# A fused attention and gated-MLP kernel: weights' high words through a leaky ReLU without a sign step, two constants in one array, products split, and a new order of issue

## The chip, the cores and the metric

The kernel runs on one core of a Trainium2 chip. The core has engines that run side by side, each with a queue of its own that is worked off in order: TensorE (PE in the profile, with PEld for its weight loads), VectorE (DVE), ScalarE (ACT), GpSimd (POOL) and SyncE (SP), which here issues nearly all DMA transfers. The metric is the time of one execution on the device in microseconds (us); lower is better.

## The reference

What is computed, for 8 batches, 8 heads, 576 positions and a head width of 64:

```python
k_p = k.reshape(B, H, 72, 8, D).mean(axis=3)          # keys and values pooled by 8
v_p = v.reshape(B, H, 72, 8, D).mean(axis=3)
attn = softmax(q @ k_p.transpose(...) / sqrt(D))
x = attn @ v_p                                         # -> (8, 576, 512)
h = gelu_tanh(x @ w_in)                                # w_in: 512 x 1024
u, v = h[..., :512], h[..., 512:]
v_n = (v - mean(v)) / sqrt(var(v) + 1e-6) * g_ln
v_s = einsum('ts,bsd->btd', w_sg, v_n) + b_sg[None, :, None]
out = x + (u * v_s) @ w_out
```

`w_in` and `w_out` come as 64-bit floats, everything else as 32-bit floats.

## The kernel before

Each product of two 32-bit operands is made of three products of their parts: an operand is rounded to a high part (`wih`, `xhl[:, 0]`, `ghi`, `vhh`) and the remainder is its low part (`wil`, `xhl[:, 1]`, `glo`, `vhl`), and high by high, high by low and low by high are added up in PSUM. The steps have letters. For batch b: A, B, C, E load keys, values, queries and leftovers; K and P pool keys and values; S makes the scores of one pair of heads (tile `e`: maximum `nmax`, exponential, sum `ssum`, division); L and T turn the scores round; V makes the attention output (tiles `x32` and `xhl`); H makes the v half of the first product (five row tiles), its gelu and its normalisation; J does the first four row tiles of H for batch 0, column group by column group; U makes the u half; W the product with `w_sg` (`wsh`, `wsl`) and the gate; O the last product; Z the store. "S1+3" in the text is step S of head pair 1, batch 3.

For batch 0 TensorE turns the scores (L176). For later batches VectorE transposes them in blocks (L509), the blocks go to HBM (`tfar`) and come back in rows (tile `al`), ScalarE rounds them to `ah` (L558), VectorE makes the remainder in `al` (L561), and V multiplies. There is one `al` buffer, so the load for the next head pair starts when V of this one is done.

Before batch 0 can be multiplied, the weights have to be split. Those of 64 bits are taken apart with integer operations (`step_w`): ScalarE scales the high word, read as a float, into `top` (L275), VectorE shifts it left by three bits (L277), puts the sign bit back (L278) and masks (L279); ScalarE casts it to the high part (L283), and L222, L224, L228 and L231 make the low part. There are twelve such steps (v0 to v3, u0 to u3, o0 to o3), each of a tile of 128x512. `load_wsg` loads `w_sg`, `b_sg` (copied to all partitions, `bbc`) and `g_ln` (`gcol`).

The list ORDER sets the order in which the steps are recorded, and with it each engine's queue: a name there advances that step to its next yield. The set OTHER names single operations that go to another engine than the usual one (a sum to VectorE instead of GpSimd, a copy to VectorE instead of ScalarE, the scores' exponential as one instruction after a subtraction on VectorE instead of ten with a bias each). Matmul outputs turn over two PSUM tiles `mps` and two `aps`.

Of the kernel before, what the change touches and what calls it, by code (L numbers as in the profile page):

```python
# [32 lines left out]
V1+0 S0+1 o0 P1+1 H1+0 V3+0 S1+1 V2+0 E0+1 H2+0 o1 A1+2 V0+0 S0+1 S0+1 H0+0 H0+0 S1+1 H3+0 H1+0 H4+0 S2+1 S1+1 S0+1
H0+0 H2+0 H3+0 S2+1 H1+0 o1 S3+1 lo1 H1+0 H1+0 o1 o1 o2 H4+0 H4+0 s3 C0+2 P2+1 P2+1 U0+0 U0+0 H4+0 K0+2 S2+1 H4+0
H3+0 o3 U1+0 U2+0 U1+0 U2+0 P2+1 o2 H3+0 S0+1 o2 H3+0 H2+0 H4+0 H2+0 o3 o2 U3+0 U3+0 S2+1 T0+1 H2+0 S3+1 S2+1 C1+2
T0+1 H4+0 o3 H3+0 S3+1 o3 H4+0 S1+1 S1+1 W0+0 W0+0 K1+2 K1+2 S3+1 W0+0 S3+1 B0+2 C3+2 T1+1 P0+2 L0+1 W1+0 P2+1 C2+2
K0+2 L0+1 W2+0 S0+2 T0+1 W1+0 W1+0 W1+0 W2+0 W2+0 S0+2 W0+0 S1+2 S0+2 L0+1 P2+1 B1+2 T0+1 W2+0 W3+0 A0+3 W3+0 W3+0
# [798 lines left out]
```

## Time and profile before

| What | us |
|---|---|
| median of three runs | 558.33 |
| lowest and highest | 555.67, 558.74 |
| the profiled execution | 558.14 |
| its span, first to last instruction | 556.4 |

So 1.74 us of the profiled execution lie outside its span. TensorE is busy for 531.2 us of the span (95%), VectorE for 420.4, ScalarE for 278.8, GpSimd for 239.6. The page's slices of the span show TensorE at 90% or more in nearly all of them from 140 us to the end, and below that in the first quarter.

### The profile page before, as it was taken

How to read it: one execution, taken by the hardware profiler on the slowest of the kernel's cores; microseconds unless marked ns; L12 is line 12 of the kernel's file. 1: busy time of each engine (PE TensorE's matmuls, PEld its weight loads, DVE VectorE, ACT ScalarE, POOL GpSimd, SP SyncE). 2: the span in 40 equal slices, each digit the busy share in tenths (PEclk: the TensorE clock that was granted, in tenths of full speed). 3: DMA queues.
4: the chain of work that ended last, by engine and by line, in shares of the span. 5: the costliest groups of instructions: out<-in, count | busy, mean ns of one | idle time of the engine just before them, and what ended most of it. 6: DMA issues, size and time to landing. Idle time of an engine off the chain costs nothing.

```text
span 556.4 us, 9530 instructions
## 1 busy us (share of the span) xinstructions
PE 531.2 (95%) x3552; PEld 500.6 (90%) x3552; DVE 420.4 (76%) x674; ACT 278.8 (50%) x569; POOL 239.6 (43%) x323
## 2 busy tenths in 40 slices
PE   3998889999999999999999999999999999999996
PEld 3976689987999999989999999989999899989996
DVE  5688999778879779787777987885878956574262
ACT  3696999455764649343554537354354354313100
POOL 4331658477366753564333642562524532232000
PEclk9998999989999999999999999999999999999998
DMA  8993304655734345325534065441341242101002
GB/s 298 339 325 96 141 2 137 192 150 138 250 100 103 88 145 205 95 64 161 152 87 135 0 184 155 132 144 46 104 130 47 44 126 89 42 1 65 1 0 107
DMA packets 43134, 67.08 MB, mean 121 GB/s; under 512 B 5776, under 2 KB 22160, under 8 KB 43088
## 3 DMA queue, kind: packets, MB, share of 16 engines
q1 hardware_dynamic: 42800, 66.03, 39.0%
q8 instruction: 28, 0.46, 0.3%
q10 hardware_dynamic: 288, 0.44, 0.2%
q14 instruction: 18, 0.15, 0.1%
HBM read 47.73 MB, written 18.73 MB: 119 GB/s over the span
## 4 chain that ended last, share of the span: by engine, by line
PE 82%; ACT 6%; DVE 5%; DMA 4%; issue 1%; SPq 1%; POOL 1%; DVEq 0%; ACTq 0%
PE mps L133 68%; PE aps L133 13%; DMA qT<-in_q 1%; DMA al<-tfar 1%; DMA kraw<-in_k 1%; ACT e L457 1%; ACT L204 1%; SPq L234 1%; DVE al L561 1%; PE aps L176 1%; DVE wsl L231 0%; ACT vg L640 0%; DVE y L509 0%; ACT top L275 0%; ACT kbd L377 0%
## 5 line engine op out<-in xcount | busy, mean ns | idle before, releaser
L133 PE MATMUL mps<-xhl,wih 128*128 128x288 f32 x512 | 89.1, 295 | 2.7 <-ACT u L681 1.7
L133 PE MATMUL mps<-wih,xhl 128*128 128x512 f32 x256 | 84.2, 399 | 0.1
L133 PEld LDWEIGHTS mps<-xhl,wih 128*128 128x128 f32 x512 | 75.0, 188 | 4.1 <-ACT u L681 2.0
L443 POOL TENSOR_TENSOR e<-e,ssum 128x720 f32<-128x720 f32 x23 | 36.1, 1570 | 52.4 <-DVE ssum L442 52.3
L133 PEld LDWEIGHTS mps<-wih,xhl 128*128 128x128 f32 x256 | 48.0, 188 | 11.6 <-DVE xhl L231 0.6
L133 PE MATMUL mps<-wsh,vhh 128*128 128x288 f32 x256 | 54.8, 295 | 0.0
L133 PE MATMUL mps<-wsl,vhh 128*128 128x288 f32 x256 | 54.7, 294 | 0.0
L133 PE MATMUL mps<-wsh,vhl 128*128 128x288 f32 x256 | 54.5, 294 | 0.0
L133 PE MATMUL mps<-xhl,wil 128*128 128x288 f32 x256 | 54.5, 294 | 0.0
L133 PE MATMUL mps<-ghi,woh 128*128 128x288 f32 x240 | 52.0, 298 | 0.0
L133 PE MATMUL mps<-glo,woh 128*128 128x288 f32 x240 | 51.2, 294 | 0.0
L133 PE MATMUL mps<-ghi,wol 128*128 128x288 f32 x240 | 51.1, 294 | 0.0
L133 PE MATMUL mps<-wil,xhl 128*128 128x512 f32 x128 | 50.6, 395 | 0.0
L647 POOL TENSOR_TENSOR rstd<-mv,eps 128x1 f32<-128x1 f32 (+1 forms) x40 | 13.1, 328 | 76.5 <-DVE mv L645 67.3
L133 PE MATMUL aps<-kbd,qT 128*128 128x144 f32 x300 | 42.7, 292 | 2.7 <-ACT e L457 1.9
L204 ACT ACT_TABLE_LOAD x35 | 44.9, 1283 | 0.6
L133 PEld LDWEIGHTS aps<-kbd,qT 128*128 128x128 f32 x300 | 40.5, 196 | 4.2 <-ACT e L457 2.3
L695 DVE SCALAR_TENSOR_TENSOR mps<-mps,gcol,bbc 128x576 f32<-128x576 f32 x32 | 26.1, 816 | 23.1 <-PE mps L133 23.1
L640 ACT ACTIVATE vg<-mps 128x512 f32<-128x512 f32 x32 | 19.1, 596 | 48.1 <-PE mps L133 43.5
L133 PEld LDWEIGHTS mps<-xhl,wil 128*128 128x128 f32 x256 | 41.0, 188 | 0.0
L133 PEld LDWEIGHTS mps<-wsh,vhl 128*128 128x128 f32 x256 | 40.9, 188 | 0.0
L133 PEld LDWEIGHTS mps<-wsh,vhh 128*128 128x128 f32 x256 | 40.9, 188 | 0.0
(170 smaller groups left out, 1319.1 us busy)
## 6 DMA issues: line engine op xcount, KB each, us to landing
qT<-in_q SPq DMA_DIRECT2D x31, 288.0 KB, 4.4
out<-x SPq DMA_DIRECT2D x31, 288.0 KB, 2.7
kraw<-in_k SPq DMA_DIRECT2D x14, 576.0 KB, 4.5
al<-tfar SPq DMA_DIRECT2D x28, 288.0 KB, 2.9
vraw<-in_v SPq DMA_DIRECT2D x14, 512.0 KB, 5.0
tfar<-y SPq DMA_DIRECT2D x56, 80.0 KB, 1.9
raw<-in_moe_w_in SPq DMA_DIRECT2D x4, 1024.0 KB, 9.5
tfar<-y SPq DMA_DIRECT2D x56, 64.0 KB, 1.8
```

The costliest lines, as they stand in the source:

```text
L133: nc.tensor.matmul(o, lhsT, rhs, start=start, stop=stop)
L176: nc.tensor.transpose(ps[:rows, i * P:(i + 1) * P], src(i), ident if i < NT - 1 else swap)
L204: nc.scalar.activation(early, eps[:, 0:1], func)
L234: queue.dma_start(o, i)
L443: (nc.gpsimd if key in OTHER else nc.vector).tensor_tensor(e, e, rec.unsqueeze(3).broadcast_to([P, NT, 2, SP]), op=ALU.mult)
L457: nc.scalar.activation(e[:, i, h], slots[i][:, h], AF.Exp, bias=nmax[:, i, h:h + 1], accum_out=ssum[:, i, h:h + 1])
L561: nc.vector.tensor_tensor(lo, al, ah.bitcast(F32), op=ALU.subtract)
L640: nc.scalar.activation(vg, o, AF.Gelu_apprx_tanh)
L647: nc.gpsimd.tensor_tensor(rstd, mv[:, 1:2], eps[:n, 1:2], op=ALU.add)
L695: nc.vector.scalar_tensor_tensor(vs, vs, gcol[:, d:d + 1], bbc.rearrange("p (a n) -> p a n", a=2), op0=ALU.mult, op1=ALU.add)
```

## The change

1. In `step_w` the scaling on ScalarE becomes a leaky ReLU (`Prelu`) whose slope for negative inputs is 2^32 times the other. The exponent then carries a bit that the shift by three puts where the sign belongs, so the sign step on VectorE is left out. The cast to the high part may go to GpSimd (`move`).
2. `b_sg` and `g_ln` come in one array (`bg`), already copied to 128 partitions, by one DMA instead of two.
3. The remainder of V (`rest`) may be made on VectorE straight from PSUM; before it was always made from the copy `x32`.
4. J makes high by high and low by high first, for all four row tiles, and high by low (`wil`) after a yield.
5. The last product of the last batch goes to two PSUM tiles instead of one, and each half is added to x right behind its matmuls.
6. ORDER and OTHER are new.

```diff
 ORDER = """
-lv0 A0+0 v0 v0 E0+0 A1+0 C0+0 v1 v1 v1 v1 v0 K0+0 lv1 B0+0 K0+0 A0+1 v3 v0 v2 S0+0 S0+0 K1+0 v3 v2 C1+0 S0+0 K1+0 v3
+C0+0 E0+0 A0+0 K0+0 K0+0 lv0 v0 C1+0 S0+0 S1+0 v0 S0+0 v1 S1+0 v0 v1 v0 A1+0 S0+0 C2+0 B0+0 S1+0 S0+0 K1+0 K1+0 B1+0
...
-    bbc = const.tile([P, S], F32, name="bbc")
-    gcol = const.tile([P, DF2 // P], F32, name="gcol")
+    both = const.tile([P, S + DF2 // P], F32, name="both")
+    bbc, gcol = both[:, 0:S], both[:, S:]
...
+    def rest(lo, x, ps, hi, key):
+        if key in OTHER:
+            nc.vector.tensor_tensor(lo.rearrange("p (a n) -> p a n", a=2), ps,
+                                    hi.rearrange("p (a n) -> p a n", a=2), op=ALU.subtract)
+        else:
+            nc.gpsimd.tensor_tensor(lo, x, hi, op=ALU.subtract)
...
-            nc.scalar.activation(top.bitcast(F32), high.bitcast(F32), AF.Copy, scale=2.0 ** -112)
+            nc.scalar.activation(top.bitcast(F32), high.bitcast(F32), AF.Prelu, scale=2.0 ** -112, alpha=2.0 ** 32)
             yield
             nc.vector.tensor_scalar(top, top, 3, None, op0=ALU.logical_shift_left)
-            nc.vector.scalar_tensor_tensor(top, high, -0x80000000, top, op0=ALU.bitwise_and, op1=ALU.bitwise_or)
             nc.vector.tensor_scalar(high, top, -0x800000, None, op0=ALU.bitwise_and)
...
-            nc.scalar.copy(hi, top)
+            move(hi, top, f"{name}{c}h")
...
-        load(bbc, b_sg.rearrange("(o t) -> o t", o=1).broadcast_to([P, S]))
-        load(gcol, g_ln.rearrange("(c p) -> p c", p=P))
+        load(both, bg)
...
-        combine(xhl[:, 1, g], x32, xhl[:, 0, g].bitcast(F32), ALU.subtract, f"V{min(b, 3)}{g}")
+        rest(xhl[:, 1, g], x32, xs, xhl[:, 0, g].bitcast(F32), f"V{min(b, 3)}{g}")
...
-        for i, o in enumerate(st["hp"]):
-            t = slice(i * P, i * P + P)
-            for j, (w, x) in enumerate(((wih, 0), (wil, 0), (wih, 1))):
-                mm(o, xhl[:, x, c, t], w[:, c, DF2:2 * DF2], c == 0 and j == 0, c == KC - 1 and j == 2)
-        yield
+        for pairs in (((wih, 0), (wih, 1)), ((wil, 0),)):
+            for i, o in enumerate(st["hp"]):
+                t = slice(i * P, i * P + P)
+                for w, x in pairs:
+                    mm(o, xhl[:, x, c, t], w[:, c, DF2:2 * DF2], c == 0 and w is wih and x == 0, c == KC - 1 and w is wil)
+            yield
...
-        ps = atile() if b == B - 1 and m % 2 else mtile()
...
             for n in range(2):
                 t = slice(HALF * n, HALF * (n + 1))
+                ps = (atile, mtile)[n]()[:, 0, 0:HALF]
...
-            for n in range(2):
-                nc.vector.tensor_tensor(x[:, n], ps[:, n, 0:HALF], x[:, n], op=ALU.add)
+                nc.vector.tensor_tensor(x[:, n], ps, x[:, n], op=ALU.add)
                 yield
             return
+        ps = atile() if b == B - 1 and m % 2 else mtile()
```

Three places show what the new order does. The first is SyncE's queue at the start; `raw` from `in_moe_w_in` is a piece of `w_in`, `kraw` are keys, `raw0` takes the leftover keys (`in_kv0`) and the values (`in_v0`) of batch 0. Before:

```order
L234 DMA raw_123<-in_moe_w_in 128x2x1024
L234 DMA kraw_125<-in_k0 128x1024
L234 DMA raw0_132<-in_kv0 64x1024
L234 DMA kraw_135<-in_k0 128x1024
L234 DMA raw_160<-in_moe_w_in 128x2x1024
L234 DMA raw0_132<-in_v0 128x1024
L234 DMA kraw_165<-in_k 128x1152
L234 DMA qT_201<-in_q 128x576
```

Now:

```order
L242 DMA raw0_124<-in_kv0 64x1024
L242 DMA kraw_127<-in_k0 128x1024
L242 DMA raw_142<-in_moe_w_in 128x2x1024
L242 DMA qT_146<-in_q 128x576
L242 DMA kraw_180<-in_k0 128x1024
L242 DMA qT_183<-in_q 128x576
L242 DMA raw0_124<-in_v0 128x1024 x2
L242 DMA raw_227<-in_moe_w_in 128x2x1024
```

The leftover keys and the first half of the keys have moved ahead of the first piece of `w_in`, and both halves of the values ahead of its second piece.

The second place is TensorE's queue at J0+0, the first products with `w_in`. Before, from S3+0 on:

```order
L133 MATMUL aps<-kbd_96,qT 128x144 x5
L133 MATMUL aps<-ah,vb 128x288
L133 MATMUL aps<-lt,vl 128x288
L133 MATMUL aps<-ah,vb 128x288
L133 MATMUL aps<-lt,vl 128x288
L133 MATMUL mps<-wih,xhl 128x512
L133 MATMUL mps<-wil,xhl 128x512
L133 MATMUL mps<-wih,xhl 128x512 x2
```

Now, from the second turn (T1+0) on:

```order
L177 MATMUL aps<-ident,e 128x128 x4
L177 MATMUL aps<-swap,e 128x128
L134 MATMUL mps<-wih,xhl 128x512 x8
L134 MATMUL aps<-ah,vb 128x288
L134 MATMUL aps<-lt,vl 128x288
L134 MATMUL aps<-ah,vb 128x288
L134 MATMUL aps<-lt,vl 128x288
```

The eight matmuls with `wih` come first, V1+0 (the four rows with `ah` and `lt`) has moved behind them, and the four matmuls with `wil` come later still.

The third place is TensorE's queue at the end of W3+0, where V of batch 1 begins (`vbh`, `vbl` are its values). Before:

```order
L133 MATMUL mps<-wth,vht 128x288 x2
L133 MATMUL mps<-wtl,vht 128x288 x2
L133 MATMUL mps<-ghi,woh 128x288 x2
L133 MATMUL mps<-ghi,wol 128x288 x2
L133 MATMUL mps<-glo,woh 128x288 x2
```

Now:

```order
L134 MATMUL mps<-wth,vht 128x288 x2
L134 MATMUL mps<-wtl,vht 128x288 x2
L134 MATMUL aps<-ah,vbh 128x288
L134 MATMUL aps<-ah,vbl 128x288
L134 MATMUL aps<-lt,vl 128x288
L134 MATMUL aps<-al,vbh 128x288
```

V0+1 has moved ahead of the first chunks of O0+0 (18 matmuls with `ghi` and `glo`), which now stand between it and V1+1: 42 matmuls there, against 30 before.

## Rows read from the trace of the kernel before

**Rows 1.** Stages: us; busy (instructions) of PE, PEld, DVE, ACT, POOL; clock, DMA share, GB/s.
```profile
8.56:38.72 30.16, 28.42 (x137) 25.08 (x138) 24.00 (x43) 20.56 (x72) 8.48 (x8) 1.00 0.98 351
38.72:69.60 30.88, 26.37 (x129) 20.71 (x127) 28.14 (x46) 25.57 (x75) 12.64 (x14) 0.94 0.42 132
69.60:85.10 15.50, 13.33 (x96) 12.87 (x97) 14.28 (x30) 15.36 (x41) 9.07 (x12) 1.00 0.01 2
85.10:128.90 43.80, 40.91 (x293) 39.74 (x292) 36.80 (x51) 25.43 (x74) 28.90 (x30) 0.96 0.58 170
128.90:551.20 422.30, 422.21 (x2902) 402.20 (x2901) 314.54 (x504) 189.28 (x307) 174.32 (x234) 1.00 0.34 100
551.20:556.40 5.20, 0.00 (x0) 0.00 (x0) 0.82 (x2) 0.00 (x0) 0.00 (x0) 0.71 0.46 170
```

**Rows 2.** Timeline of TensorE: start, duration, instructions; in brackets the idle time before.
```profile
38.72 0.61 PE L133 MATMUL mps<-wih,xhl 128*128 128x512 f32 x1
...
69.60 0.80 PE L133 MATMUL mps<-xhl,wih 128*128 128x288 f32 x4 [0.49 <-ACT vg L640]
...
85.11 0.42 PE L133 MATMUL mps<-wsh,vhh 128*128 128x288 f32 x2
```

**Rows 3.** Waits of TensorE from 38.7 to 129 us: total, times, longest.
```profile
PE aps L176 <- DVE e L443: 2.0, 1, 2.0
PE aps L133 <- ACT e L457: 1.9, 1, 1.9
PE aps L133 <- ACT ah L558: 1.8, 1, 1.8
PE mps L133 <- ACT u L681: 1.7, 1, 1.7
```

**Rows 4.** Stages again, as in 1: the two stretches with a low clock.
```profile
43.90:48.40 4.50, 4.47 (x20) 3.50 (x21) 4.40 (x7) 1.31 (x3) 1.62 (x2) 0.62 0.54 175
...
112.40:116.00 3.60, 3.40 (x14) 3.18 (x15) 3.08 (x6) 2.93 (x6) 1.40 (x1) 0.59 0.05 6
```

**Rows 5.** Chain that ended last, at the start: start, duration, what.
```profile
8.56 4.74 PE mps L133 x20
```

**Rows 6.** Timeline of ScalarE at the start, columns as in 2.
```profile
6.15 0.68 ACT L275 ACTIVATE top<-raw 128x512 f32<-128x512 f32 x1 [4.07 <-DMA raw<-in_moe_w_in]
```

**Rows 7.** Groups of VectorE: instructions xcount | busy us, mean ns | idle before.
```profile
L733 DVE TENSOR_TENSOR x<-mps,x 128x576 f32<-128x576 f32 x30 | 22.4, 749 | 15.6 <-PE mps L133 15.4
...
L231 DVE TENSOR_TENSOR xhl<-x,xhl 128x576 fp32r<-128x576 f32 x17 | 15.1, 888 | 2.6 <-ACT x L211 2.4
...
L278 DVE SCALAR_TENSOR_TENSOR top<-raw,top 128x512 int32<-128x512 int32 x12 | 8.3, 693 | 0.4
```

**Rows 8.** Groups of ScalarE, columns as in 7.
```profile
L204 ACT ACT_TABLE_LOAD x35 | 44.9, 1283 | 0.6
...
L453 ACT ACTIVATE e<-e 128x720 f32<-128x720 f32 x25 | 19.8, 801 | 7.5 <-DVE e L448 7.2 <-POOL kraw L358 0.2
...
L457 ACT ACTIVATE e<-aps,nmax 128x72 f32<-128x72 f32 x60 | 18.2, 335 | 0.6 <-DVE nmax L486 0.6
...
L275 ACT ACTIVATE top<-raw 128x512 f32<-128x512 f32 x12 | 7.8, 672 | 4.5 <-DMA raw<-in_moe_w_in 4.5
```

**Rows 9.** Chain that ended last, from 104 to 130 us, columns as in 5.
```profile
106.73 4.90 DMA al<-tfar
...
112.44 0.77 DVE al L561
...
116.93 2.38 PE mps L133 x18
...
122.42 2.98 DMA al<-tfar
...
126.18 1.73 DVE al L561
```

**Rows 10.** Timeline of VectorE at the end, columns as in 2.
```profile
551.23 0.82 DVE L721 TENSOR_TENSOR x<-aps,x 128x288 f32<-128x288 f32 x2 [2.40 <-PE aps L133]
```

More of the change, by code (lines that the diff above doesn't have):

```diff
@@ L33 @@
[L33 to L37, printed above, removed]
@@ new lines @@
+S2+2 T2+1 T3+1 S1+2 V1+1 O1+0 O1+0 S1+2 V0+1 S2+2 O2+0 O2+0 C1+3 T2+1 S0+2 V2+1 A1+3 K1+3 S2+2 O3+0 O3+0 V2+1 V2+1
+V2+1 O2+0 T3+1 T3+1 T3+1 B0+2 S3+2 S0+2 V3+1 P0+2 V3+1 O3+0 T0+2 C0+3 V3+1 H0+1 S2+2 T1+2 S3+2 H0+1 H0+1 S3+2 S3+2
+H1+1 H1+1 H1+1 B1+3 Z0+0 H0+1 V1+1 H2+1 H3+1 H0+1 T0+2 A0+3 H2+1 H1+1 H0+1 H3+1 H1+1 V3+1 H4+1 H1+1 T0+2 H2+1 S2+2
+Z2+0 U0+1 H4+1 H4+1 U0+1 H4+1 H3+1 T0+2 T3+2 S3+2 P2+2 U1+1 K0+3 K0+3 L0+2 P2+2 H2+1 H3+1 H4+1 H2+1 Z3+0 S0+3 S0+3
+U1+1 U2+1 H3+1 H3+1 P2+2 L0+2 P2+2 U3+1 U2+1 P1+3 Z1+0 H2+1 L0+2 L0+2 V0+2 T1+2 S1+3 C3+3 T2+2 H4+1 U3+1 H4+1 H4+1
@@ new lines @@
+S1+3 T1+2 T1+2 V0+2 W0+1 W0+1 V1+2 V1+2 T2+2 S0+3 C2+3 L0+2 T2+2 W1+1 V0+2 W1+1 K1+3 W2+1 E0+3 T2+2 V2+2 S0+3 C0+4
+S2+3 S1+3 W3+1 W1+1 T3+2 V2+2 V1+2 V1+2 W2+1 W1+1 V2+2 T3+2 T3+2 V3+2 B0+3 S1+3 W3+1 W0+1 W0+1 V3+2 V3+2 H0+2 H1+2
+H0+2 V0+2 T0+3 S2+3 P0+3 T0+3 H1+2 W2+1 W2+1 W3+1 O0+1 A1+4 W3+1 O0+1 C1+4 H1+2 S3+3 O1+1 O0+1 O1+1 H0+2 P2+3 S0+3
+O2+1 A0+4 S3+3 H0+2 V2+2 S2+3 P2+3 V3+2 K1+4 H1+2 H1+2 O2+1 H1+2 O1+1 S3+3 B1+4 H2+2 K1+4 K0+4 O2+1 S2+3 S3+3 Z2+1
+H2+2 P2+3 B0+4 H0+2 H0+2 H3+2 S1+3 K0+4 H4+2 H2+2 S0+4 H3+2 T1+3 U0+2 S2+3 H4+2 H4+2 S3+3 C3+4 U1+2 H3+2 L0+3 H4+2
@@ new lines @@
+T0+3 P2+3 H4+2 S1+4 S0+4 U0+2 U1+2 Z0+1 P2+3 H2+2 H2+2 H4+2 O3+1 H2+2 L0+3 L0+3 O3+1 P0+4 L0+3 A0+5 T0+3 H3+2 V0+3
+T1+3 T1+3 U2+2 U2+2 O3+1 H3+2 Z3+1 T2+3 H3+2 S0+4 S1+4 T1+3 U3+2 U3+2 V1+3 T2+3 L0+3 Z1+1 H4+2 T2+3 H4+2 W0+2 T3+3
+P1+4 V0+3 V0+3 T2+3 E0+4 W0+2 W1+2 V2+3 V1+3 S0+4 T3+3 C1+5 W1+2 W0+2 K0+5 K0+5 W0+2 S1+4 W1+2 T3+3 T3+3 W2+2 W2+2
+W3+2 W3+2 W1+2 C2+4 V3+3 V2+3 S2+4 V3+3 V3+3 W2+2 V1+3 V2+3 H0+3 W2+2 C0+5 H0+3 S2+4 S2+4 V1+3 S3+4 H0+3 S1+4 H1+3
+H1+3 H2+3 T0+4 H0+3 O0+2 H2+3 S1+4 T0+4 S0+4 H0+3 H0+3 S3+4 T1+4 W3+2 H3+3 H1+3 S3+4 W3+2 O0+2 H3+3 O0+2 H2+3 S0+5
@@ L90, with tile_pooled_attn_gmlp @@
+p20 p21 p31 s0d s3d s4d u0a u0d u0m u1a u1d u1m u2a u2m u3d u3h u3m v0a v1m v2h v2m x22 z13 z20 z21 z22 z23 z24 z31
+z32 z34
 """.split())
 @with_exitstack
-def tile_pooled_attn_gmlp(ctx: ExitStack, tc: tile.TileContext, q, k0, kv0, v0, k, v, vleft, w_in, g_ln, w_sg, b_sg, w_out, out):
+def tile_pooled_attn_gmlp(ctx: ExitStack, tc: tile.TileContext, q, k0, kv0, v0, k, v, vleft, w_in, w_sg, bg, w_out, out):
     nc = tc.nc
@@ L462, in total, with root @@
             nc.vector.tensor_reduce(out=ssum, in_=e, axis=AX.X, op=ALU.add)
+    def root(rstd, var, key):
+        n = rstd.shape[0]
+        nc.gpsimd.tensor_tensor(rstd, var, eps[:n, 1:2], op=ALU.add)
+        nc.gpsimd.tensor_tensor(rstd, rstd, mhalf[:n], op=ALU.pow)
     def scaled(vg, mv, rstd, key):
@@ L646, in step_H @@
         rstd = per.tile([P, 1], F32, name="rstd", tag=f"rstd{i}")[:n]
-        nc.gpsimd.tensor_tensor(rstd, mv[:, 1:2], eps[:n, 1:2], op=ALU.add)
-        nc.gpsimd.tensor_tensor(rstd, rstd, mhalf[:n], op=ALU.pow)
+        root(rstd, mv[:, 1:2], f"r{min(b, 3)}{i}")
         yield
```

98 lines of the change are left out of this document (44 added, 54 removed).

## The prediction

> **What bounds the kernel now.** I read the stages first. From 128.9 us to the last matmul at 551.2 us TensorE is busy for 422.21 of 422.30 us at a granted clock of 1.00 (2.4 GHz) [rows 1]: there its own work is the time, and the change leaves every matmul in place (3345 before and now by the order). So the change can only win ahead of 128.9 us and behind 551.2 us. Ahead of it, the first matmul starts at 8.56 us [rows 5], J0+0 at 38.72, U0+0 at 69.60 and W0+0 at 85.11 [rows 2]. TensorE is idle for 30.16 - 28.42 = 1.74 us between the first matmul and J0+0, for 4.51 us from there to U0+0, for 2.17 to W0+0 and for 2.89 to 128.9 [rows 1]. I read next what ended those waits: 2.0 us for VectorE's division of e ahead of T, 1.9 for ScalarE's exponentials ahead of S, 1.7 for ScalarE's gelu of u, 1.8 for `ah` of V1+1 [rows 3]. Two of these, of 2.0 and 1.8 us, are followed by a stretch with the clock at its lower level (1.2 GHz) for a part: 0.62 over 4.50 us and 0.59 over 3.60 us [rows 4], which costs another 0.38 x 4.50 = 1.7 and 0.41 x 3.60 = 1.5 us. Last I looked at who is full: between J0+0 and W0+0, 46.4 us, VectorE is busy for 28.14 + 14.28 = 42.4 us (91%) and ScalarE for 25.57 + 15.36 = 40.9 (88%) [rows 1]. TensorE waits there for two engines that are nearly full themselves.
>
> **The change, part by part.** The sum is made against the profiled execution, 558.14 us, of which 1.74 lie outside the span; the median of the runs is 558.33, so the two can be taken as the same.
>
> Start. The first matmuls need the leftover keys (256 KB), the first half of the keys (512 KB), and S0+0 needs the query (288 KB). Before, 1024 KB of `w_in` stood ahead on SyncE's queue and landed by 6.15 us [rows 6]; the keys came behind them, at 8.56 [rows 5]. Now these 1056 KB come first. They are as much as that first transfer, so I take 6.3 us: a gain of 2.3 us (1.5 to 2.5). `w_in` comes later, but its high part is wanted by J0+0 only, some 28 us on, and its first piece now has one piece of 1056 KB in front instead of none, at 351 GB/s [rows 1] a delay of 3 us: hidden by those 28. The values now land ahead of the second piece of `w_in`, which c = 2 wants, behind J1.
>
> Up to J0+0 VectorE loses six sign steps, 6 x 0.693 = 4.2 us [rows 7] of its 24.00 [rows 1], and J0 begins with eight matmuls that don't want `wil`. Of the 1.74 us idle I take back 1.2 (0 to 1.7). Together **-3.5 us** at J0+0, with equal work in front. V1+0 has moved behind it, so the record will show J0+0 about a microsecond earlier still.
>
> From J0+0 to W0+0. By TensorE's waits alone, 2.0 + 1.9 + 1.7 us and the clock's 1.7 could go, 7.3 in all; against it J0's second matmul now wants the low part of x, which stands on VectorE behind a sum of keys (`kp`), so I put 1.6 us back: 46.4 - 5.7 = 40.7 us. But VectorE alone has more to do than that. It loses the other six sign steps there, 4.2 us [rows 7]; by the order it gets two sums of keys, two row sums and some steps of the splits that stood ahead of J0+0 before, and gives up two scalings and two remainders of vg and the remainders of P2+1, each of 0.4 to 1.3 us, which I estimate at 3.5 us more, net. That leaves 42.4 - 4.2 + 3.5 = 41.7 us. At its share of now, 91%, the stage takes 45.8 us (-0.6); at 97%, 43.0 (-3.4). ScalarE has slack: 20 of the exponentials with a bias go, 20 x 18.2/60 = 6.1 us, for two whole ones of 0.80, and two of the table loads of 1.283 move behind W0+0 [rows 8]. I take the middle of VectorE's two, **-2.0 us**.
>
> The price of the new ScalarE form: its row is the scaling with Copy, 0.672 us x12 [rows 8], same shape and operands, and I take it unchanged. The program has 38 table loads instead of 36 and none beside the new form. The Trainium skill (ScalarE: Activation LUTs, section Table sets: the hidden batching unit) says that cheap functions such as relu, copy, identity and abs are in every table set; it does not name the leaky ReLU, so by its list a load could be wanted each time. The Trainium skill (ScalarE activation tables: per-element evaluation and per-set limits, section What a function is on this engine) give 1283 ns a load, and the row agrees with 1283. That case is a rival below.
>
> Remainder of V from PSUM: 13 of 32 go that way. No row shows it; its nearest is the sum x<-mps,x of the same size with one operand in PSUM, 0.749 us, against 0.888 for xhl<-x,xhl [rows 7]; so 0.70 to 0.89, and I take 0.75. It need not wait for the copy to x. The cast of a high part on GpSimd (two of twelve) has no row: between 0.3 and 1.4 us, hidden, since the first product with that part comes several microseconds later. The Trainium skill (GPSIMD Engine Reference, section 1. Specifications) says that GpSimd shares its SBUF interfaces with VectorE, with contention for VectorE instructions with two SBUF inputs. By this the form from PSUM would win 13 x 0.139 = 1.8 us of VectorE, and the twelve operations that GpSimd gains ahead of W0+0 would lengthen VectorE's others; the mean of 0.888 beside 0.749 agrees with the first, no row here shows the second.
>
> One DMA instead of two for the constants costs nothing: they are first wanted by the gate of W0+0.
>
> From W0+0 to 128.9. V0+1's end lets the load of `al` go at 106.73; the remainder is ready at 112.44 + 0.77 = 113.2: 6.5 us. For the third it is 122.42 to 127.9, 5.5 us [rows 9]. Eighteen matmuls take 2.38 us [rows 9], 0.132 each: the 30 matmuls behind V0+1 hide 4.0 us, the 42 of now 5.5. So the first wait falls from about 2.5 to 1.0 us, and I take the clock's fall behind it as gone for the most part, 1.3 of 1.5 (a wait of 1.7 us for u has a clock of 1.00 all through its stage [rows 1, 3]). The waits at the other two I leave. **-2.8 us** (-4.2 to +1).
>
> From there to the last matmul there is nothing to win; for the two table loads and the moved work I add **+0.5 us** (0 to +4).
>
> The end. Both additions of the last product now wait for TensorE's end (idle 2.40 us) and take 0.82 us together [rows 10]; stores queue behind the first half's. Now the first half is added 18 matmuls sooner, its store and the others go out while TensorE works, and one half and one small store remain of the 5.20 us [rows 1]. One addition less is 0.4 us, the queue less I estimate at 0.9: **-1.3 us** (-0.4 to -1.8).
>
> Sum: -3.5 - 2.0 - 2.8 + 0.5 - 1.3 = -9.1 us, 558.14 - 9.1 = **549.0 us**.
>
> **Rivals.** *More comes through* (16%): VectorE reaches 97%, the idle time before J0+0 goes, all of V's waits go, no loss later: -4.2 - 3.4 - 4.2 - 1.8 = -13.6, 544.5 us; for it, TensorE's clock would not fall at all. *VectorE stays the bound* (15%): GpSimd has twelve more operations ahead of W0+0 and VectorE waits for its results or is slowed by it, so W0+0 comes where it came, at 85 us; then -2.8 + 0.5 - 1.3 = -3.6, 554.5 us. For it: 91% now; against it, twelve sign steps less. *Slower: a wait at each change of batch* (6%). TensorE has no slack from 128.9 on. If the new order put a result too late there, each idle stretch of 2.0 us with the clock's 1.7 behind it costs 3.7 us; from the third of seven batches on, the gain of 9.1 is gone, and with all seven it is 549.0 + 26 = 575 us. Against it: the PSUM tiles turn over there in the same pattern as before, and VectorE was busy for 314.5 of 422 us. *The leaky ReLU wants its own table* (2%): two loads for each of twelve steps, 24 x 1.283 = 30.8 us on ScalarE, which has 76.5 - 61.5 = 15.0 us idle from the first matmul to W0+0 [rows 1]: 549.0 + 15.8 = 565 us. Against it: the program has no such loads.
>
> **How the numbers follow.** The forecast, 546 to 553 us, has 61%, and the four rivals 16, 15, 6 and 2. The range of 8 in 10 reaches into the first two rivals: 541.5 to 555.0 us. A measurement of this kernel tells 0.5% (2.8 us) from no change, so faster means below 555.5: forecast and first rival and about half of the second, 0.84; same 0.08; slower 0.08.
>
> **What would show it.** The first matmul at 6.0 to 6.6 us; J0+0 near 34; W0+0 near 79.5; the new activation at 0.67 us with no load beside it; the remainder from PSUM at 0.70 to 0.76; VectorE at 93 to 95% between J0+0 and W0+0; under 1.5 us of wait at V1+1 and no low clock there; the stretch from V3+1 to the last matmul within 2 us of 422; 4 us from the last matmul to the end. W0+0 at 83 us or later, or idle time of TensorE behind 130 us, would make it wrong.

## The result and the profile after

The changed kernel takes 551.9 us (median; 551.1 to 552.1) against 558.33 (555.67 to 560.25) of the kernel before: a ratio of 0.989 with a 95% interval of 0.9855 to 0.9925, so 1.1% faster, and inside the 546 to 553 us that I forecast. Its profiled execution took 552.02 us with a span of 550.3; that is 6.1 us less than the profiled execution before, where I had forecast 9.1.

The stages first, cut at the same places as [rows 1]: first matmul, J0+0, U0+0, W0+0, first product of batch 1, last matmul. Columns: us; busy (instructions) of PE, PEld, DVE, ACT, POOL; granted clock, DMA share, GB/s.

```profile
0.00:7.85 7.85, 0.00 (x0) 0.03 (x1) 0.21 (x1) 1.49 (x2) 6.15 (x26) 1.00 0.71 222
7.85:38.09 30.24, 27.30 (x129) 24.10 (x130) 20.25 (x30) 15.41 (x44) 11.73 (x12) 0.89 0.72 277
38.09:67.34 29.25, 26.54 (x139) 21.04 (x137) 27.25 (x48) 25.24 (x60) 18.03 (x22) 1.00 0.71 232
67.34:81.60 14.26, 13.30 (x100) 12.84 (x98) 12.78 (x27) 14.17 (x40) 10.14 (x13) 1.00 0.07 26
81.60:120.25 38.65, 37.53 (x282) 36.79 (x281) 33.23 (x51) 23.87 (x88) 18.37 (x21) 1.00 0.48 139
120.25:546.15 425.90, 424.91 (x2914) 403.77 (x2912) 311.52 (x496) 215.67 (x437) 143.41 (x205) 1.00 0.34 102
546.15:550.30 4.15, 0.00 (x0) 0.00 (x0) 0.46 (x1) 0.00 (x0) 0.00 (x0) 1.00 0.60 225
```

Two pieces of work stand in another stage than before, and have to be taken out before stages are compared. V1+0 is now behind J0+0; it takes 43.10 - 41.16 = 1.9 us. One S step, ten matmuls (1.1 us), is now behind the first product of batch 1. TensorE's timeline (start, duration, instructions, idle time before):

```profile
7.85 1.86 PE L134 MATMUL mps<-pool,kraw 128*128 128x16 f32 x8 [7.85 <-DMA kraw<-in_k]
...
38.09 0.49 PE L134 MATMUL mps<-wih,xhl 128*128 128x512 f32 x1
39.43 1.89 PE L134 MATMUL mps<-wih,xhl 128*128 128x512 f32 x7 [0.85 <-DVE xhl L236]
41.16 0.65 PE L134 MATMUL aps<-ah,vb 128*128 128x288 f32 x2
...
43.10 0.60 PE L177 MATMUL aps<-ident,e 128*128 128x128 f32 x4
...
81.60 0.43 PE L134 MATMUL mps<-wsh,vhh 128*128 128x288 f32 x2
```

With that, the steps of the forecast against the profile (before: [rows 1, 2]; its first product of batch 1 is at 128.73 us, and the steps are rounded to 0.1):

| Step | worked out | forecast | measured |
|---|---|---|---|
| up to J0+0 | 38.09 + 1.9 - 38.72 | -3.5 | +1.3 |
| J0+0 to W0+0 | (43.51 - 1.9) - 46.39 | -2.0 | -4.8 |
| W0+0 to the first product of batch 1 | (38.65 + 1.1) - 43.62 | -2.8 | -3.9 |
| from there to the last matmul | (425.90 - 1.1) - 422.47 | +0.5 | +2.3 |
| last matmul to end | 4.15 - 5.20 | -1.3 | -1.05 |
| sum | | -9.1 | -6.1 |

So the sum was 3 us off, and it hides two larger misses at either end (the start and the steady part, 6.6 us together) that two middle steps made good in part (3.9 us). TensorE's waits ahead of 120 us (total, times, longest) show both sides:

```profile
PE aps L134 <- ACT kbd L383: 1.9, 1, 1.9
PE mps L134 <- ACT vg L652: 0.9, 1, 0.9
PE mps L134 <- ACT u L692: 0.9, 1, 0.9
PE mps L134 <- DVE xhl L236: 0.8, 1, 0.8
...
PE aps L134 <- DMA qT<-in_q: 0.7, 1, 0.7
PE aps L134 <- DVE lt L551: 0.4, 1, 0.4
```

The four waits of 1.7 to 2.0 us of [rows 3] are gone: the gelu of u costs 0.9 instead of 1.7, the division ahead of T and the exponentials ahead of S after J0+0 nothing, and `ah` of V1+1 nothing, with a clock of 1.00 from 38 us to the end. What is new is a wait of 1.9 us for `kbd`, ahead of J0+0.

The three single operations I had priced came out as priced. Groups of ScalarE and VectorE (count | busy us, mean ns | idle before):

```profile
L205 ACT ACT_TABLE_LOAD x37 | 47.5, 1283 | 0.6
...
L283 ACT ACTIVATE top<-raw 128x512 f32<-128x512 f32 x12 | 7.9, 670 | 0.6 <-POOL wil L232 0.5
...
L236 DVE TENSOR_TENSOR xhl<-aps,xhl 128x576 fp32r<-128x576 f32 x13 | 9.7, 745 | 2.0 <-ACT x L212 2.0
```

The leaky ReLU takes 0.670 us (Copy 0.672, [rows 8]) and no table load stands beside any of the twelve; the record has 37 loads against 35, and it has 37 too with the Copy put back (next section), so the two more come with the order. The remainder from PSUM takes 0.745 us (0.75 assumed).

### The profile page after: what moved, and what is told of

The parts are those of the page before. It is cut to its first block, busy times and chain, and to the rows that moved or that the text cites. A ratio compares the mean times of both kernels' runs of the same rounds, so it can differ in the third digit from the quotient of the medians.

```text
span 550.3 us, 9577 instructions
## 1 busy us (share of the span) xinstructions
PE 529.6 (96%) x3552; PEld 498.6 (91%) x3552; DVE 405.7 (74%) x651; ACT 295.9 (54%) x668; POOL 207.8 (38%) x295
## 4 chain that ended last, share of the span: by engine, by line
PE 77%; ACT 8%; DVE 6%; DMA 5%; issue 2%; SPq 1%; POOL 0%; DVEq 0%; ACTq 0%
PE mps L134 66%; PE aps L134 11%; ACT e L463 2%; DMA al<-tfar 1%; SPq L242 1%; ACT L205 1%; DMA kraw<-in_k 1%; DMA vraw<-in_v 1%; DMA qT<-in_q 1%; DVE al L572 1%; ACT vg L482 1%; DVE kp L361 1%; DVE vp L361 1%; DVE nmax L497 1%; ACT vhh L212 1%
## 5 line engine op out<-in xcount | busy, mean ns | idle before, releaser
L134 PE MATMUL mps<-wih,xhl 128*128 128x512 f32 x256 | 81.6, 398 | 0.8 <-DVE xhl L236 0.8
L239 POOL TENSOR_TENSOR xhl<-x,xhl 128x576 fp32r<-128x576 f32 x19 | 27.8, 1469 | 79.3 <-ACT x L212 79.3
L134 PE MATMUL mps<-ghi,woh 128*128 128x288 f32 x244 | 53.5, 299 | 0.0
L449 POOL TENSOR_TENSOR e<-e,ssum 128x720 f32<-128x720 f32 x23 | 33.1, 1437 | 52.1 <-DVE ssum L448 46.9
L134 PE MATMUL mps<-ghi,wol 128*128 128x288 f32 x244 | 52.5, 295 | 0.0
L134 PE MATMUL mps<-wil,xhl 128*128 128x512 f32 x128 | 48.8, 397 | 0.0
L472 POOL TENSOR_TENSOR rstd<-mv,eps 128x1 f32<-128x1 f32 (+1 forms) x40 | 11.0, 274 | 98.5 <-DVE mv L657 93.4
L134 PEld LDWEIGHTS aps<-kbd,qT 128*128 128x128 f32 x300 | 40.3, 194 | 4.4 <-ACT kbd L383 2.0
L706 DVE SCALAR_TENSOR_TENSOR mps<-mps,both 128x576 f32<-128x576 f32 x32 | 26.1, 816 | 20.0 <-PE mps L134 19.9
```

The costliest lines, as they stand in the source:

```text
L134: nc.tensor.matmul(o, lhsT, rhs, start=start, stop=stop)
L239: nc.gpsimd.tensor_tensor(lo, x, hi, op=ALU.subtract)
L449: (nc.gpsimd if key in OTHER else nc.vector).tensor_tensor(e, e, rec.unsqueeze(3).broadcast_to([P, NT, 2, SP]), op=ALU.mult)
L472: nc.gpsimd.tensor_tensor(rstd, var, eps[:n, 1:2], op=ALU.add)
L706: nc.vector.scalar_tensor_tensor(vs, vs, gcol[:, d:d + 1], bbc.rearrange("p (a n) -> p a n", a=2), op0=ALU.mult, op1=ALU.add)
```

## Experiments

Each time is compared with runs of the kernel before on the same chip; the changed kernel's ratio is 0.989 (0.9855 to 0.9925). J0+0 and W0+0 are from the profiles.

| Kernel | us | ratio to before (95%) | J0+0 | W0+0 |
|---|---|---|---|---|
| changed | 551.9 | 0.9890 (0.9855, 0.9925) | 38.1 | 81.6 |
| sign step back | 558.4 | 1.0009 (0.9992, 1.0026) | 37.0 | 85.7 |
| before, with the leaky ReLU | 557.3 | 0.9988 (0.9968, 1.0009) | 39.7 | 84.5 |
| keys pooled ahead of S1+0 | 556.1 | 0.9967 (0.9952, 0.9982) | 40.3 | 83.9 |
| exponentials of S1+0 whole | 551.7 | 0.9888 (0.9866, 0.9910) | 35.8 | 79.2 |
| both edits at the start | 555.0 | 0.9947 (0.9924, 0.9971) | 39.8 | 83.1 |
| splits earlier | 552.8 | 0.9909 (0.9883, 0.9935) | 36.6 | 80.1 |
| w_in ahead of the keys | 554.5 | 0.9958 (0.9932, 0.9984) | 38.3 | 81.7 |
| J in the old pattern | 552.5 | 0.9912 (0.9881, 0.9943) | 35.9 | 80.4 |
| remainder of V from x32 | 554.2 | 0.9932 (0.9909, 0.9955) | 36.5 | 81.5 |
| vht's cast on VectorE | 551.5 | 0.9873 (0.9844, 0.9903) | 36.4 | 80.0 |
| old form of the end | 555.2 | 0.9942 (0.9918, 0.9967) | 36.0 | 79.7 |
| three edits together | 549.3 | 0.9848 (0.9822, 0.9875) | 35.8 | 79.7 |

One thing is to be read off this table before the experiments. The kernels with vht's cast moved and with the old form of the end differ from the changed kernel only far behind W0+0, those with J in the old pattern and with the remainder from x32 only behind V0+0's products, and still the profiles of these four have J0+0 at 36.4, 36.0, 35.9 and 36.5 us where the changed kernel's has 38.1. From the first matmul to J0+0 it is 28.6 to 29.3 us in the four and 30.2 in the changed kernel's. So one profile gives J0+0 to 2 us and no better: the first step of the table above lies between -1.0 and +1.3 us. With vht's cast moved and with the old form of the end the stretch from the first product of batch 1 to the last matmul is 1 us longer, so that part of the difference is given back.

### The sign step and the order

My theory was that VectorE is the bound from J0+0 to W0+0. Two runs take the sign step and the order apart: the changed kernel with the sign step put back (all other parts of the change stay with the order), and the kernel before with the leaky ReLU alone.

```diff
-            nc.scalar.activation(top.bitcast(F32), high.bitcast(F32), AF.Prelu, scale=2.0 ** -112, alpha=2.0 ** 32)
+            nc.scalar.activation(top.bitcast(F32), high.bitcast(F32), AF.Copy, scale=2.0 ** -112)
...
             nc.vector.tensor_scalar(top, top, 3, None, op0=ALU.logical_shift_left)
+            nc.vector.scalar_tensor_tensor(top, high, -0x80000000, top, op0=ALU.bitwise_and, op1=ALU.bitwise_or)
```

> Edit: the changed kernel with the sign step put back (the scaling is a Copy again, VectorE ORs the sign bit in), order and all else as changed. Twelve steps of 0.69 us on VectorE, six of them between J0+0 and W0+0 (4.2 us), the others ahead of it. My theory: VectorE is the bound from J0+0 to W0+0, where the change gained 3.9 us of TensorE's waits; with the sign step most of that is lost: W0+0 at 85 us instead of 81.6, 555 to 556 us. Rival: VectorE's time freed there is slack, and the new order made the gain: W0+0 within 1 us of 81.6, 552 to 553 us.

Measured: 558.4 us, as slow as before. From J0+0 to W0+0 it takes 48.7 us instead of 43.5. Its stages there, and TensorE's longest waits:

```profile
36.99:72.50 35.51, 28.64 (x139) 22.23 (x137) 33.97 (x55) 26.93 (x63) 19.48 (x22) 0.95 0.61 198
72.50:85.73 13.23, 13.23 (x99) 12.85 (x98) 12.88 (x28) 11.67 (x35) 10.45 (x12) 1.00 0.03 10
```

```profile
PE mps L134 <- ACT vg L653: 2.3, 1, 2.3
PE mps L134 <- DVE xhl L236: 2.2, 2, 1.3
```

The sign steps alone in the same stretch (us; busy time and instructions of VectorE in them; clock, DMA share, GB/s):

```profile
36.99:85.73 48.74, 7.58 (x8) 0.96 0.45 147
```

So eight of the twelve sign steps stand in this stage in the new order, and not six as I had written: the order has moved two splits behind J0+0. VectorE is busy for 46.85 of 48.74 us (96%): full. Without the eight steps it is busy for 27.25 + 12.78 = 40.0 of 43.5 (92%). They cost 7.6 us of VectorE and 5.2 us of time: two thirds of their length comes through. The waits for V's remainders at J grow from 0.8 to 2.2 us. What the other four cost ahead of J0+0 can't be told: it comes 30.2 us after the first matmul, within the 28.6 to 30.2 of the profiles without them.

The other half, the kernel before with the leaky ReLU alone:

```diff
-            nc.scalar.activation(top.bitcast(F32), high.bitcast(F32), AF.Copy, scale=2.0 ** -112)
+            nc.scalar.activation(top.bitcast(F32), high.bitcast(F32), AF.Prelu, scale=2.0 ** -112, alpha=2.0 ** 32)
...
-            nc.vector.scalar_tensor_tensor(top, high, -0x80000000, top, op0=ALU.bitwise_and, op1=ALU.bitwise_or)
```

> Edit: the kernel before, with the leaky ReLU in place of the scaling and without the sign step; order and all else as before. My theory (VectorE the bound, 91% busy from J0+0 to W0+0): twelve operations less give 2 to 4 us, W0+0 at 81 to 83 us, 554.5 to 556 us. Rival (the order is what counts): in the old order VectorE waits for the same other results, W0+0 stays within 1 us of 85.1 and the time at 557.5 to 558.3 us. In both the new activation takes 0.67 us and the table loads stay 35 in the record.

Measured: 557.3 us, 0.9988 (0.9968 to 1.0009): no difference that can be told from none. The rival is right here. Its waits from J0+0 to W0+0:

```profile
PE aps L176 <- DVE e L442: 2.0, 1, 2.0
PE aps L133 <- ACT e L456: 1.9, 1, 1.9
PE mps L133 <- ACT u L680: 1.7, 1, 1.7
```

They are those of [rows 3] to the tenth, although VectorE has 4 us less to do in that stage (26.18 + 12.20 us busy of 44.8). The stage is 1.6 us shorter than before (44.8 against 46.4) for another reason: TensorE is busy for 1.7 us less, at a granted clock of 1.00 all through, where it was 0.62 for 4.5 us before [rows 4]. The part of it with the waits of 2.0 and 1.9 us, columns as in the stages above:

```profile
39.65:68.94 29.29, 24.67 (x130) 19.69 (x128) 26.18 (x43) 25.50 (x75) 12.68 (x14) 1.00 0.49 141
```

I read from this that in the old order each of these waits follows from a chain of dependent steps, not from how much work the engines have. So neither half is worth anything alone: the new order without the free VectorE gives 1.0009, the free VectorE in the old order 0.9988, and both 0.989. "VectorE is the bound" holds for the new order only.

### The start

In the changed kernel TensorE waits ahead of S2+0. ScalarE's and TensorE's timelines:

```profile
19.48 0.32 ACT L463 ACTIVATE e<-mps,nmax 128x72 f32<-128x72 f32 x1 [0.66 <-DVE nmax L497]
...
22.16 0.36 ACT L463 ACTIVATE e<-mps,nmax 128x72 f32<-128x72 f32 x1
...
22.45 0.60 ACT L383 ACTIVATE kbd<-mps 64x144 f32<-64x144 f32 x2
```

```profile
13.36 5.14 PE L134 MATMUL mps<-kbd,qT 128*128 128x144 f32 x20 [0.78 <-issue]
...
19.83 1.07 PE L134 MATMUL mps<-pool,kraw 128*128 128x16 f32 x8
...
23.11 2.77 PE L134 MATMUL aps<-kbd,qT 128*128 128x144 f32 x10 [1.90 <-ACT kbd L383]
...
26.74 6.90 PE L134 MATMUL mps<-raw,pool 128*128 128x256 f32 x26
...
34.02 1.39 PE L134 MATMUL aps<-kbd,qT 128*128 128x144 f32 x10
```

The copy of the second pooled keys to `kbd` stands behind ten exponentials. Behind the wait the granted clock is at its lower level (1.2 GHz), 0.50 in both of these stretches:

```profile
23.10:25.90 2.80, 2.79 (x12) 2.78 (x13) 1.97 (x3) 0.60 (x1) 2.72 (x3) 0.50 0.96 373
25.90:28.60 2.70, 2.70 (x10) 2.34 (x10) 2.19 (x3) 1.62 (x3) 1.00 (x3) 0.50 1.00 379
```

I took these 5 us for the whole miss, and tried to remove them in three ways. First the pooling ahead of S1+0's scores:

```diff
-... S0+0 S1+0 v0 S0+0 v1 S1+0 v0 v1 v0 A1+0 S0+0 C2+0 B0+0 S1+0 S0+0 K1+0 K1+0 B1+0
+... S0+0 v0 S0+0 v1 v0 v1 v0 A1+0 S0+0 C2+0 B0+0 S0+0 K1+0 K1+0 S1+0 S1+0 S1+0 B1+0
```

> Edit: the changed kernel, with the scores of S1+0 (and their maximum and exponentials) put behind the pooling of the second half of the keys (K1+0), as they stood before. In the changed kernel TensorE is idle for 1.9 us ahead of S2+0 at 23.1 us, because the copy of the pooled keys to kbd stands on ScalarE behind the ten exponentials of S1+0; the granted clock behind that wait is 0.50 over 3.9 us and 0.63 over the next 3.0, which costs another 3.1 us. My theory: this one wait ate the gain of the start, 5.0 us; without it the clock stays at 1.00 from 21 to 30 us, J0+0 comes near 33 to 34 us instead of 38.1, and the time is 547 us (changed kernel 551.9). Rival: the wait stands in front of a later limit (values and w_in land only at 16.6 to 19.1 us, VectorE is idle until 14 us and has to catch up), so that J0+0 stays at 37 to 38 us and the time at 551 to 552.

Measured: 556.1 us, slower by 0.8% of the time. Both theories fell. The wait at 20 us is gone, but TensorE waits once, for longer, further on (waits ahead of J0+0, then VectorE's timeline):

```profile
PE aps L172 <- DVE e L444: 3.8, 1, 3.8
```

```profile
22.77 0.91 DVE L492 TENSOR_REDUCE nmax<-mps 128x10 f32<-128x720 f32 x1 [2.57 <-PE mps L129]
```

VectorE now waits 2.57 us for the scores of S1+0, and everything behind shifts, up to the division of e for S2+0. That division keeps its scratch values in the PSUM tile of S2's scores, and the turn of `el` wants that tile. So VectorE's chain S1, S2, division is the next limit, a little behind TensorE's.

Second, the order of the changed kernel, with `m01` added to OTHER, so that S1+0's exponentials are one instruction of 0.80 us:

> Edit: the changed kernel, with the exponentials of S1+0 as one instruction behind a subtraction on VectorE (one name more in OTHER); the order stays. ScalarE's ten with a bias took 3.0 us (19.48 to 22.4), the whole one takes 0.80 and the subtraction and row sum 0.91 and 0.90 on VectorE. My theory (the wait at 21 us and the low clock behind it cost the start 5.0 us): kbd is ready near 21.3 us, the wait falls under 1 us, the clock stays up, the time falls to 547 to 548 us. Rival (a later limit on VectorE): VectorE gets 1.8 us more to do ahead of J0+0, so J0+0 stays at 38 or comes later, 552 to 553 us.

Measured: 551.7 us, the same time. The wait for `kbd` is down to 0.7 us (1.0 to 2.2 in the profiles of the unchanged start), and the way from the first matmul to J0+0 is 28.7 us, which the unchanged start has too in some profiles. The granted clock falls again, and it does so ahead of the wait, which is from 20.2 to 20.8 us:

```profile
19.50:20.00 0.50, 0.50 (x4) 0.47 (x3) 0.50 (x2) 0.29 (x1) 0.00 (x0) 0.61 1.01 373
20.00:20.50 0.50, 0.17 (x1) 0.08 (x1) 0.50 (x2) 0.28 (x1) 0.00 (x0) 0.50 0.20 74
...
21.00:25.00 4.00, 4.00 (x16) 3.47 (x17) 3.83 (x9) 0.60 (x2) 3.16 (x3) 0.50 0.92 344
```

From 17.3 us on TensorE had run twenty pooling matmuls of 16 and 8 columns, and it is busy with the last of them when the clock falls. Third, both edits at once:

> Edit: both edits at the start at once: K1+0 ahead of the scores of S1+0, and the exponentials of S1+0 whole. With the first alone, S1+0's result came too late for the turn of el, and TensorE was idle for 3.8 us at 30 us (time 556.1); with the second alone the wait at 20 us fell to 0.7 us, but the granted clock still stood at 0.50 from 20 to 25 us (551.7). Theory 1: what costs the start is the low clock behind the small pooling matmuls and the wait at 20 us; with both edits the clock is 1.00 there and e of S1+0 is ready by 26 us, J0+0 comes at 33.5 to 34.5 us (35.8 with the second alone) and the time is 549.5 to 551. Theory 2: VectorE sets J0+0, since it is idle until 14 us and then has to do everything that stands ahead of J0's second matmul: J0+0 at 36 to 38 us, time 551.5 to 553.

Measured: 555.0 us, J0+0 at 39.8: later than either theory had it. The turn of `el` waits 3.1 us for the same division; the order alone does that, with whole exponentials or without. Its rows from S2+0 on say also that the low clock was not what I took it for:

```profile
21.78 2.61 PE L125 MATMUL aps<-kbd,qT 128*128 128x144 f32 x10
...
24.80 5.67 PE L125 MATMUL mps<-raw,pool 128*128 128x256 f32 x26
```

The granted clock is 1.00 there, and the ten matmuls take 2.61 us, nearly the 2.77 of the changed kernel at 0.50. TensorE has this slow pace in its first score matmuls in every kernel here, whatever the clock column says (more on it in the last section). The 26 matmuls behind them do run faster than in the changed kernel (5.67 us against 6.90), but the pooling ahead of them is slower (1.89 us for eight matmuls of 16 columns, against 1.07 at 19.83 us there). From the first matmul to the end of the 26 it takes 23.8 us here, 23.1 with the order alone and 25.8 in the changed kernel: 2.0 and 2.7 us less, 1.9 of it the wait. So of the 3.1 us that I had put on the clock at most 0.8 came with the wait removed, and the wait of 3.1 us at the turn of `el` takes back more than the gain.

Then I asked whether VectorE's late start is what counts: it is idle for 10.2 us until 13.98, where before it split weights from 6.86 us on.

```diff
-C0+0 E0+0 A0+0 K0+0 K0+0 lv0 v0 C1+0 S0+0 S1+0 v0 S0+0 v1 S1+0 v0 v1 v0 ...
+C0+0 E0+0 A0+0 K0+0 lv0 v0 v0 v1 v1 K0+0 C1+0 S0+0 S1+0 S0+0 S1+0 v0 v0 ...
```

> Edit: the changed kernel, with the first two steps of v0 and v1 (scaling on ScalarE, shift and mask on VectorE) ahead of the first copy to kbd and of the maximum of S0+0. VectorE is idle until 14 us in the changed kernel (until 6.9 in the kernel before), and from 5 to 41 us it is idle for 13.5 us against 8.4 before; 0.87 us of its work, which now stands behind the maximum of S1+0 at 19.4 us, goes into that idle time. Theory 1 (VectorE sets when J0+0 comes, so what the sign steps saved was used up by its later start): J0+0 comes 0.9 us earlier than in other profiles of this start (36.0 to 38.1, so 35 to 36.5) and the time falls by 0.3 to 0.9 us, to 551.0 to 551.6. Theory 2 (TensorE with its low clock from 21 to 28 us sets it): J0+0 stays at 36 to 38 and the time at 551.9.

Measured: 552.8 us, no gain. VectorE starts at 10.96 us, and waits as long later (2.52 us ahead of the first maximum, 1.58 ahead of S2's): theory 2. I read from these four that TensorE's chain over `kbd` leads, and that VectorE follows it closely: in the two with the pooling first the wait moved to the turn of `el` (3.8 and 3.1 us for 1.9). For the other two the profiles can't tell a gain at J0+0 from none.

Last, the order of the transfers: `lv0` moved to the front of ORDER, so that the first piece of `w_in` goes ahead of the keys again.

> Edit: the changed kernel with the first piece of w_in again ahead of all else on SyncE's queue; the rest of the order stays. My theory: the new order of transfers brought little, since the keys landed at 7.7 us with w_in behind them against 8.4 with w_in ahead, and VectorE had no work until 14 us. So J0+0 and W0+0 stay within 1 us of the changed kernel's (38.1 and 81.6) and the time within 1 us of 551.9. Rival (the keys first are worth what I forecast, 2.3 us): the first matmul at 8.5 us, all behind it 1 to 2 us later, 553 to 554 us.

Measured: 554.5 us, the rival: 0.9958, 0.7% of the time above the changed kernel's ratio. The first matmul comes at 9.68 us. J0+0 at 38.3 and W0+0 at 81.7 us lie within 1 us of the changed kernel's profile, as in my theory, but J0+0 lies 1.8 to 2.4 us behind the four other profiles of its start.

```profile
9.68 1.86 PE L129 MATMUL mps<-pool,kraw 128*128 128x16 f32 x8 [9.68 <-DMA kraw<-in_k]
```

So the keys in front are worth some 2 us at the first matmul. Over the profiles of the new start it comes at 6.7 to 7.9 us, not at 6.3: by 7.85 us 7.85 x 222 = 1,740 KB have been moved (stages above), where the transfers issued up to the keys have 1,056. The transfers queued behind them are served at the same time.

### Behind 120 us

TensorE has small waits in the changed kernel where the kernel before had hardly any, mostly at the same places. The largest is in W0+2, for `vht`, the last row tile of v. ScalarE's and VectorE's timelines ahead of it:

```profile
210.24 0.67 ACT L569 CAST ah<-al 128x576 fp32r<-128x576 f32 x1 [5.61 <-DMA al<-tfar]
...
215.62 0.61 ACT L212 CAST vht<-vg 64x512 fp32r<-64x512 f32 x1
```

```profile
216.26 0.69 DVE L674 TENSOR_TENSOR vht<-vg,vht 64x512 fp32r<-64x512 f32 x1 [3.78 <-ACT vht L212]
```

The cast of `vht` stands behind `ah`, which waits for the load of `al`, and behind two table loads. TensorE's next matmul comes 0.48 us late here, and 1.0 to 1.3 us late in the profiles of eight of the variants. Adding `g24` to OTHER gives that cast to VectorE:

> Edit: the changed kernel with one name more in OTHER: from batch 2 on the cast of the last row tile (vht) is done by VectorE instead of ScalarE. In the changed kernel TensorE waits at 216.4 us (in W0+2) for vht; its cast stands on ScalarE behind the rounding of al, which waits for a load of al of 4.0 us, and behind two table loads. My theory: the stretch behind 120 us lost about 2 us more than before at five such places, and this one (0.5 to 1.3 us in the profiles of the changed kernel and its variants) goes: 0.3 to 1.0 us less, 551.0 to 551.6. Rival: the time taken back there is lost again at the next wait for al (229.7 us): 551.9 to 552.2.

Measured: 551.5 us; the wait for `vht` is gone, and another one of 1.1 us has come, at 263 us, for VectorE's `vg`. In time neither theory can be told from the other.

### The other parts

The end as before, in one PSUM tile with both additions behind the last matmul (the first half's store moves behind its addition):

> Edit: the changed kernel with the last product of the last batch as before: both halves in one PSUM tile, both additions behind the last matmul; the store of the first half moves behind its addition, the other stores stay where they are. In the profiles the time from the last matmul to the end fell from 5.2 us to 4.2. My theory: this edit alone gives that back, 5.1 to 5.4 us again, so 552.9 us (changed kernel 551.9). Rival: the end is set by the last store's own time, and 4.2 to 4.5 us stay, 552 us.

Measured: 555.2 us (the interval of its ratio overlaps that of the changed kernel by a little); the last matmul's end to the end takes 7.3 us instead of 4.15, more than the 5.20 of before. Timeline of VectorE at the end of the changed kernel, then of this one:

```profile
543.80 0.46 DVE L731 TENSOR_TENSOR x<-aps,x 128x288 f32<-128x288 f32 x1 [0.83 <-PE aps L134]
...
546.18 0.46 DVE L731 TENSOR_TENSOR x<-mps,x 128x288 f32<-128x288 f32 x1 [0.82 <-PE mps L134]
```

```profile
545.41 0.81 DVE L727 TENSOR_TENSOR x<-aps,x 128x288 f32<-128x288 f32 x2
```

In the changed kernel the first half is added 2.4 us ahead of the second, and its store goes. In this one four stores queue up on SyncE behind 545.95 us. My edit keeps the new order of the last products, in which others stand behind this one, so it prices the old form in the new order (3 us), not the change itself, for which 4.15 against 5.20 is the number.

J's products row tile by row tile, all ahead of its first yield:

> Edit: the changed kernel with J's products in the old pattern: high by high, high by low and low by high row tile by row tile, all ahead of J's first yield. V1+0 and the turns then stand behind twelve matmuls instead of eight. I put 1.6 us on J's second matmul waiting for the low part of x (measured 0.85 in the changed kernel). Theory: in the old pattern the third matmul waits for the same low part, so the split is worth under 0.5 us and the time stays within 0.6 us of 551.9. Rival: the four matmuls with the low part of w_in wait for its remainder on GpSimd, 1 us or more: 553 us or above.

Measured: 552.5 us, as expected; TensorE waits 0.6 us for the low part of x where it waited 0.8. From J0+0 to W0+0 it takes 44.5 us instead of 43.5 in this profile, so the split may be worth up to 1 us there; the time doesn't show it.

The remainder of V always from the copy:

```diff
-        rest(xhl[:, 1, g], x32, xs, xhl[:, 0, g].bitcast(F32), f"V{min(b, 3)}{g}")
+        combine(xhl[:, 1, g], x32, xhl[:, 0, g].bitcast(F32), ALU.subtract, f"V{min(b, 3)}{g}")
```

> Edit: the changed kernel with the remainder of V always made from the copy x32, on VectorE for the same 13 of 32 as before it was made on VectorE or GpSimd. The form from PSUM took 0.745 us (x13) in the changed kernel, the form from x32 0.888 (x17) in the kernel before: 13 x 0.143 = 1.9 us of VectorE and the wait for ScalarE's copy (0.65 us) ahead of each. Theory: at J0+0 and J1+0 TensorE waits for that remainder, so the copy's wait counts there; 0.3 to 1.0 us more, 552.2 to 552.9. Rival: hidden, 551.9 within 0.3.

Measured: 554.2 us, 2.3 more than the changed kernel, above what I expected; the intervals of the two ratios overlap from 0.9909 to 0.9925. From J0+0 to W0+0 it takes 45.0 us instead of 43.5, the longest of all profiles of this order with the leaky ReLU (43.3 to 44.5 in the others). TensorE's waits there:

```profile
PE mps L134 <- ACT vg L652: 1.1, 1, 1.1
PE mps L134 <- DVE xhl L232: 1.0, 1, 1.0
```

The remainder had a term of at most 1.8 us of VectorE's time in the prediction and none of its own in the sum. In the full stage it counts on the path: the two waits are 0.2 us longer each than in the changed kernel, and one of 0.5 us for `xta` is new; the rest of the 1.5 us has no row.

Part 2 of the change, the two constants in one array, was not tried alone. Last, three edits together: early splits, whole exponentials of S1+0, `vht` on VectorE.

> Edit: three edits together on the changed kernel: the early splits, the whole exponentials of S1+0, and vht's cast on VectorE. Alone, the second gave 551.7 and the third 551.5 us (changed kernel 551.9). Theory 1 (what is gained in one place is a wait at the next one): 551.0 to 551.7 us. Theory 2 (the gains add up): J0+0 near 35, W0+0 near 78.5, 550 us or below.

Measured: 549.3 us (547.6 to 551.4), the fastest of all, 2.6 us below the changed kernel; the two intervals overlap by a little. Alone the three gave 552.8, 551.7 and 551.5, so the sum of the parts was nothing and together they gave something; why, the profiles show only in part. Theory 2 had the right time, but by another way: J0+0 at 35.8 and W0+0 at 79.65 are no earlier than with one of the edits. Against the single edits the gain shows behind W0+0: 38.6 us to the first product of batch 1, where the exponentials and the early splits alone have 39.9, and from there 425.1 us to the start of the last matmul, against 426.1, 426.8 and 427.8 with one edit each. The changed kernel itself has 38.65 and 425.6, so against it 2.0 of the 2.5 us between the two profiles lie ahead of W0+0, where one profile tells no better than 2 us.

## Why the prediction was right or wrong

**The time:** 551.9 us lies in the 546 to 553 of the forecast, 2.9 us above its 549.0. That is in part luck: the start and the stretch behind the first product of batch 1 were 6.6 us worse than forecast, and the two steps between them 3.9 us better.

**Right:** that VectorE is what the change relieves and that its sign steps count in the stage J0+0 to W0+0; the price of the leaky ReLU and that no table load comes with it; the remainder from PSUM; V1+1, which no longer waits (42 matmuls cover the load of `al`, and the clock stays at 1.00); the end, 4.15 us against "4 us".

**The start, -3.5 forecast, +1.3 measured (-1.0 to +1.3 over the profiles of this start), is the step that failed.** In the changed kernel's profile its 4.8 us are made up as follows. The first matmul came at 7.85 us, not 6.3 (1.5 us; 6.7 to 7.9 over the profiles), because I let the keys have the whole rate of the transfers; the ones behind them shared it. I took back 1.2 us of TensorE's 1.74 us of idle time, and it rose to 30.24 - 27.30 = 2.94 (2.4 us). And TensorE is busy for 27.30 us, 29.2 with V1+0, against 28.42 before (0.8 us): behind the wait its pace is low. The wait comes from a queue that I had not walked through: by moving S1+0's scores ahead of the second pooling, the order put ten exponentials ahead of a copy to `kbd` on ScalarE. I had written of each moved step what TensorE and VectorE do, and left out ScalarE there. But the runs that remove this wait are no faster, so it is not the whole cause: VectorE's chain up to the division stands close behind it. And I let the six sign steps saved ahead of J0+0 count as part of the gain. In the new order only four would stand there, and no run shows a gain from them: from the first matmul to J0+0 it takes 28.6 to 30.2 us in the profiles of this start, against 30.16 - 1.9 = 28.3 before for the same products.

**J0+0 to W0+0, -2.0 forecast, -4.8 measured.** The mechanism was the one in the text, as the run with the sign step shows, and the size off: I let VectorE get 3.5 us of other work back and so be busy for 41.7 us; it is busy for 40.0, at 92% where I had taken 91 to 97. TensorE's idle time there fell from 6.7 us to 3.7; the other 1.8 us are busy time, with a clock of 1.00 where it had been 0.62 for 4.5 us. This part need not come from the change, since the kernel before with the leaky ReLU alone had it with the old waits in place. The bound by waits, 40.7 us, which I had put aside for VectorE's, was within 1 us of the 41.6 measured.

**From W0+0, -2.8 forecast, -3.9 measured.** The first wait for `al` went whole, and the one of 0.8 us at 127 us, which I had left, went too; two small ones (0.4 for `lt`, 0.7 for a query) came. Here too part of the gain is the clock, 1.00 instead of 0.96.

**Behind that, +0.5 forecast (0 to +4), +2.3 measured.** I had named the rival of a new wait at each change of batch at 3.7 us each, and looked for idle stretches of 2 us. What came are some six of 0.2 to 0.5 us (up to 1.3 in the variants), with a granted clock of 1.00 throughout. I had written that idle time of TensorE behind 130 us would make the forecast wrong: it came, 1.0 us of it, and the forecast of the time held.

**The rivals.** *VectorE stays the bound* is what the run with the sign step shows: W0+0 at 85.7 us, as the rival had it at 85. I had put "twelve sign steps less" against it, and that was what decided. *The leaky ReLU wants its own table* is excluded by the groups above. *Slower at each change of batch* came at a tenth of its size: TensorE does wait for late results behind 130 us, but at some six places in all and with no fall of the clock. The record has 3552 matmuls in both kernels, not the 3345 of the prediction; that their number stays the same holds.
